# Attention and feed-forward kernel: third q, second x and third o put into the wait for the second chunk of w1, unread matmuls moved, work of batches 3 to 7 up to six slots sooner

## Chip, cores, metric

One core of one Trainium2 chip. The metric is the device time of one execution in microseconds (us); the median of several runs is quoted, with lowest and highest. The span of a profile is a little shorter than the time of the same run, so spans are compared with spans and times with times.

## The reference

```python
kv  = einsum('bhsd,bhse->bhde', k, v)              # 8 batches, 8 heads, 576 rows, d = 64
o   = einsum('bhsd,bhde->bhse', q, kv)
o   = o / sqrt(mean(o*o, -1) + 1e-6) * g_norm      # per head
x   = o.transpose(0, 2, 1, 3).reshape(8, 576, 512)
xn  = (x - mean(x)) / sqrt(var(x) + 1e-6) * g_ln
out = x + relu(xn @ w_ch1) @ w_ch2                 # w_ch1 512 x 2048, w_ch2 2048 x 512
```

## The kernel before

Almost all of the time is the two products with w_ch1 ("first product", line 401) and w_ch2 ("second product", line 417). Each main tile of 128 rows needs q turned (d on the partitions), o = q kv, square, sum, root, y, x, a centred and scaled x (xc), and xc turned, before the first product of its batch. All of that small work is hung on an agenda of slots: `tick()` is called at the start of each group of matmuls of the products, 16 slots for each product of a batch, and runs what is due. In the traces below the engines keep to the order in which the program emits their instructions, even where later work is ready (PE while it waits until 17.89 us, DVE with its evictions at 136.67 us in batch 4), so a slot decides what stands behind what. In the names used here y is o divided by its root, x is y times g_norm, and an eviction is DVE's step that reads a finished bank of the second product and writes the output tile (o_sb, line 422).

The opening of the span, with the unread matmuls (`fill`), put in so that PE has work where it would otherwise wait: In the first trace of before eight of the first 24 start about 427 ns apart and the others 216 ns apart; the record of a granted clock of 1.00 begins between the two, at 4.55 us.

```python
def turn_first(i, pool, tag):                 # q of tile i of batch 0 -> transposed
    tp = pool.tile([128, HP, 128], bf16, tag=tag, name="tp")
    n = turn_groups(tp, i, 0, H)
    nc.scalar.copy(qts[0][:, i, :, :n], tp[:, :, :n])

def fill(n):                                  # results are never read
    for _ in range(n):
        p1 = ps2.tile([128, 512], f32, tag="p2", name="p1")
        nc.tensor.matmul(p1, lhsT=fill_sb[:, :128], rhs=fill_sb, start=True, stop=True)
        del p1
# ... cut ...
fill(24)
kv_first()                                    # kv of batch 0, two halves of the heads
t = [main_tile(0, i) for i in range(4)]
# ... cut ...
half_turn(0); half_o(0, 0); half_turn(1); half_o(1, 0); half_o(0, 1)
# ... sums of squares, roots ...
t[0].o_g(ps1, "p1"); t[1].o_g(ps1, "p1")
fill(5)
t[0].x_g(); t[1].root()
# ... cut ...
halves_turn(0, halves_xc(0), ps_out, "ops")
t[1].x_g()
xc1 = list(halves_xc(1))
# ... cut ...
at(0, lambda: turn_first(2, ps_m, "misc"))              # third q
at(2, lambda: halves_turn(1, xc1, ps_out, "ops"))       # second x
at(2.1, o2); at(2.2, x2)                                # third tile
at(4, lambda: turn_first(3, ps_m, "misc"))
at(5, lambda: t[3].o()); at(5.5, x3)
at(6, lambda: t[2].turn(True))
# ... cut ...
at(11, lambda: t[3].turn(True))
```

The loads are issued in one queue in this order: v (two halves), q's lower half (two), first chunk of w1, q's upper half, then the second, third and fourth chunk of w1. The first chunk suffices for the group of 16 matmuls of slot 0; the group of slot 1 needs the second chunk, those of slots 2 and 3 the second x.

For the later batches (slots relative to s = 32 b, where the first product of batch b begins):

```python
for b in range(3, B):
    s = 32 * b                                # b = 3 has its own slots 47, 57, 57.5
    at(s - 60, lambda b=b: load_batch(b, qts[b - 1][...]))
    at(s - 39, lambda b=b: kv_of(b))
    at(s - 38, lambda b=b: turn_q_dma(b))     # pack q on DVE, transposing load
    for j in range(J):
        o = s - 28 + (0, 4, 9, 13)[j]
        plan_tile(o, lambda b=b, j=j: main_tile(b, j), o + 6, False)  # o; y, x, xc at o+2
    if b % 2:
        plan_tile(s - 8, lambda b=b: rem_tile(b), s - 2, False)
    at(s + 14, lambda b=b: rstd_of(b))
```

## Time and profile before

Time: 297.01 us median (296.92 to 297.04, 3 runs). The profiled run took 295.8 us.

| | before, first profile |
|---|---|
| span | 293.9 us |
| PE busy | 282.0 us, 96% |
| first product of batch 0 begins | 16.02 us |
| second product of batch 0 begins | 34.72 us |
| from there to the end | 259.17 us |

From the page of before (busy time with share and count by engine, then the granted clock in 40 slices of the span, 9 meaning 90% or more):

```profile
span 293.9 us, 5779 instructions
PE 282.0 (96%) x2296; PEld 159.7 (54%) x2321; DVE 149.9 (51%) x334; ACT 157.9 (54%) x342; POOL 40.8 (14%) x68
...
PEclk9999999999999999999999999999999999999999
```

PE is the limit, at full clock. Only its waits can be won. The timeline of PE in the opening (start us, duration us, engine, line, operation, output<-input, shapes, count, and in brackets the idle time ahead and what ended it):

```profile
14.96 0.68 PE L539 MATMUL tp<-identity,xc 128*128 128x128 bf16 x4 [1.49 <-DVE xc L530]
15.65 0.44 PE L183 MATMUL tp<-identity,q_in 64*64 64x64 bf16 x16
16.02 1.07 PE L401 MATMUL p<-xT_blk,w_sb 128*128 128x128 bf16 x16
17.89 1.07 PE L401 MATMUL p<-xT_blk,w_sb 128*128 128x128 bf16 x16 [0.80 <-DMA w_sb<-in_moe_w_ch_dram]
18.79 0.39 PE L539 MATMUL tp<-identity,xc 128*128 128x128 bf16 x4
19.90 0.38 PE L259 MATMUL o_ps<-kv_pack,qt 128*128 128x128 bf16 x4 [0.72 <-ACT xT_blk L540]
20.12 1.95 PE L401 MATMUL p<-xT_blk,w_sb 128*128 128x128 bf16 x32
...
34.72 4.48 PE L417 MATMUL p<-w_sb,m 128*128 128x512 bf16 x19
```

PE waits 0.80 us at 17.89 for the second chunk of w1, and right behind it does work that did not need that chunk: it turns the second x (18.79), waits 0.72 us for ACT, and makes the third o (19.90).

In the batches, DVE and PE around the second product of batch 4 show a wait that recurs in batches 3 to 7:

```profile
134.35 0.69 DVE L291 TENSOR_TENSOR y<-o_ps,inv 128x512 f32<-128x512 f32 x1
135.07 0.69 DVE L310 SCALAR_TENSOR_TENSOR x_blk<-y,g_norm_sb 128x512 f32<-128x512 f32 x1
...
136.00 0.75 DVE L320 SCALAR_TENSOR_TENSOR xc<-x_blk,st_blk,g_ln_sb 128x512 bf16<-128x512 f32 x1
136.67 1.40 DVE L422 SCALAR_TENSOR_TENSOR o_sb<-p,rstd,x_blk 128x512 f32<-128x512 f32 x2
```

```profile
137.47 1.02 PE L417 MATMUL p<-w_sb,m 128*128 128x512 bf16 x4 [0.46 <-DVE o_sb L422]
```

DVE works through y, x and xc of the next batch before it gets to two evictions (o_sb, line 422) in a row. The third tile of the second product needs the bank of the first one, so PE stands still for 0.46 us.

### The profile page before, as it was taken

How to read it: one execution, taken by the hardware profiler on the slowest of the kernel's cores; microseconds unless marked ns; L12 is line 12 of the kernel's file. 1: busy time of each engine (PE TensorE's matmuls, PEld its weight loads, DVE VectorE, ACT ScalarE, POOL GpSimd, SP SyncE). 2: the span in 40 equal slices, each digit the busy share in tenths (PEclk: the TensorE clock that was granted, in tenths of full speed). 3: DMA queues.
4: the chain of work that ended last, by engine and by line, in shares of the span. 5: the costliest groups of instructions: out<-in, count | busy, mean ns of one | idle time of the engine just before them, and what ended most of it. 6: DMA issues, size and time to landing. Idle time of an engine off the chain costs nothing.

```text
span 293.9 us, 5779 instructions
## 1 busy us (share of the span) xinstructions
PE 282.0 (96%) x2296; PEld 159.7 (54%) x2321; DVE 149.9 (51%) x334; ACT 157.9 (54%) x342; POOL 40.8 (14%) x68
## 2 busy tenths in 40 slices
PE   8779999999999999999999999999999999999995
PEld 3469855996569744444444444444444444444444
DVE  5747018936995766568246863692378600220022
ACT  3457755885569832782189327930694266017500
POOL 8523510022014000500050005000000000000000
PEclk9999999999999999999999999999999999999999
DMA  7999999459679935994899259987501520131033
GB/s 214 202 206 204 200 203 196 109 95 181 130 143 162 155 70 115 162 196 72 164 167 169 32 107 162 202 85 145 107 18 37 118 61 0 38 71 36 0 73 72
DMA packets 63290, 35.84 MB, mean 122 GB/s; under 512 B 30748, under 2 KB 58268, under 8 KB 63264
## 3 DMA queue, kind: packets, MB, share of 16 engines
q0 software_dynamic: 28016, 17.76, 43.0%
q1 hardware_dynamic: 34736, 16.99, 28.6%
q10 hardware_dynamic: 512, 0.72, 0.7%
q8 instruction: 18, 0.29, 0.4%
q14 instruction: 8, 0.07, 0.1%
HBM read 36.71 MB, written 9.44 MB: 157 GB/s over the span
## 4 chain that ended last, share of the span: by engine, by line
PE 70%; DVE 11%; ACT 6%; DMA 6%; issue 4%; POOL 1%; DVEq 0%; SPq 0%; POOLq 0%
PE p L401 37%; PE p L417 28%; DMA w_sb<-in_moe_w_ch_dram 4%; DVE x_blk L310 3%; DVE y L291 3%; PE kv_ps L234 2%; PE o_ps L259 2%; DMA qt<-q_p 2%; ACT m L404 2%; DVE o_sb L422 1%; DVE xc L320 1%; ACT sq L265 1%; ACT dev L328 1%; DVE ss L286 1%; ACT rms L296 1%
## 5 line engine op out<-in xcount | busy, mean ns | idle before, releaser
L401 PE MATMUL p<-xT_blk,w_sb 128*128 128x128 bf16 (+2 forms) x1015 | 131.2, 285 | 1.3 <-DMA w_sb<-in_moe_w_ch_dram 0.8
L417 PE MATMUL p<-w_sb,m 128*128 128x512 bf16 (+2 forms) x592 | 128.3, 367 | 2.6 <-DVE o_sb L422 0.9
L404 ACT ACTIVATE m<-p 128x512 bf16<-128x512 f32 x144 | 84.8, 596 | 59.1 <-PE p L401 57.7
L401 PEld LDWEIGHTS <-w_sb 128*128 128x128 bf16 x1024 | 78.6, 98 | 45.6 <-DMA w_sb<-in_moe_w_ch_dram 1.0
L417 PEld LDWEIGHTS <-m 128*128 128x128 bf16 x608 | 56.7, 98 | 61.4 <-issue 1.5
L422 DVE SCALAR_TENSOR_TENSOR o_sb<-p,rstd,x_blk 128x512 f32<-128x512 f32 (+2 forms) x38 | 26.9, 718 | 40.7 <-PE p L417 35.3
L328 ACT ACTIVATE dev<-x_blk,st_blk 128x512 f32<-128x512 f32 x36 | 25.8, 716 | 20.0 <-DVE st_blk L314 20.0
L286 DVE TENSOR_REDUCE ss<-sq 128x8 f32<-128x512 f32 x34 | 23.2, 682 | 25.8 <-ACT sq L265 25.7
L320 DVE SCALAR_TENSOR_TENSOR xc<-x_blk,st_blk,g_ln_sb 128x512 bf16<-128x512 f32 x34 | 25.6, 752 | 1.2
L291 DVE TENSOR_TENSOR y<-o_ps,inv 128x512 f32<-128x512 f32 x34 | 23.5, 692 | 3.4 <-DVE inv L303 0.5
L265 ACT ACTIVATE sq<-o_ps 128x512 f32<-128x512 f32 x34 | 20.2, 595 | 8.9 <-PE o_ps L259 8.9
L310 DVE SCALAR_TENSOR_TENSOR x_blk<-y,g_norm_sb 128x512 f32<-128x512 f32 x34 | 23.5, 692 | 1.2
L410 DVE RECIPROCAL rstd<-rstd 128x4 f32<-128x4 f32 x9 | 1.5, 172 | 39.7 <-ACT rstd L409 39.7
L303 DVE RECIPROCAL inv<-rms 128x8 f32<-128x8 f32 x36 | 7.2, 201 | 22.6 <-ACT rms L296 22.6
L98 POOL COPY gate<-qt 1x1 bf16<-1x1 bf16 x5 | 0.9, 178 | 122.2 <-DMA qt<-q_p 122.2
L296 ACT ACTIVATE rms<-ss,eps_sb 128x8 f32<-128x8 f32 x36 | 10.7, 297 | 9.3 <-DVE ss L286 8.6
L259 PEld LDWEIGHTS <-qt 128*128 128x128 bf16 (+1 forms) x152 | 9.9, 100 | 8.8 <-issue 2.5
L259 PE MATMUL o_ps<-kv_pack,qt 128*128 128x128 bf16 (+1 forms) x152 | 13.3, 220 | 0.8 <-ACT xT_blk L540 0.7
L196 PE MATMUL p<-fill_sb 128*128 128x512 bf16 x29 | 8.2, 445 | 1.2 <-DVE eps_sb L137 1.2
L237 ACT CAST kv_pack<-kv_ps 64x256 bf16<-64x256 f32 x7 | 2.6, 366 | 8.9 <-PE kv_ps L234 8.8
L328 ACT ACTIVATION_READ_ACCUMULATOR dev<-x_blk,st_blk 128x1 f32 x36 | 6.8, 189 | 0.0
L234 PEld LDWEIGHTS <-k_in 128*64 128x64 bf16 x280 | 5.4, 112 | 2.6 <-issue 2.5
(78 smaller groups left out, 119.8 us busy)
## 6 DMA issues: line engine op xcount, KB each, us to landing
out_dram<-o_sb SPq DMA_DIRECT2D x70, 128.0 KB, 2.4
w_sb<-in_moe_w_ch_dram POOLq DMA_DIRECT2D x8, 512.0 KB, 14.0
k_in<-in_k_dram POOLq DMA_DIRECT2D x7, 320.0 KB, 5.4
v_in<-in_v_dram POOLq DMA_DIRECT2D x7, 320.0 KB, 8.0
q_in<-in_q_dram POOLq DMA_DIRECT2D x7, 320.0 KB, 10.4
q_in<-in_q_dram POOLq DMA_DIRECT2D x8, 256.0 KB, 11.3
k_in<-in_k_dram POOLq DMA_DIRECT2D x7, 256.0 KB, 6.7
v_in<-in_v_dram POOLq DMA_DIRECT2D x7, 256.0 KB, 8.9
```

The source lines that it names most:

```text
L259: nc.tensor.matmul(flat[rows, hp * 128:(hp + 1) * 128], lhsT=lhsT_of(hp), rhs=kvp[:, hp, :], start=True, stop=True)
L265: nc.scalar.activation(self.sq_t, self.o_ps, func=AF.Square)
L286: nc.vector.tensor_reduce(self.ss, self.sq_t, axis=AX.X, op=ALU.add)
L291: nc.vector.tensor_mul(self.y_t, self.o_ps, self.inv().to_broadcast([128, H, D]))
L296: nc.scalar.activation(self.r, self.ss, func=AF.Sqrt, scale=1.0 / D, bias=eps_sb)
L310: nc.vector.scalar_tensor_tensor(x_blk[:, ts].rearrange("p (h d) -> p h d", h=H), in0=self.y_t, scalar=1.0, in1=g_norm_sb.to_broadcast([12 ...
L320: nc.vector.scalar_tensor_tensor(self.xc_t, in0=x_blk[:, self.ts], scalar=st[:, 1, self.ts:self.ts + 1], in1=g_ln_sb, op0=ALU.add, op1=ALU ...
L328: nc.scalar.activation(dev, x_blk[:, ts], func=AF.Square, bias=st[:, 1, ts:ts + 1], accum_out=st[:, 2, ts:ts + 1])
L401: nc.tensor.matmul(p1[:, i, :], lhsT=w1_sb[:, kk, de * 128:(de + 1) * 128], rhs=blk[2][:, kk, sl], start=(kk == 0), stop=(kk == nK - 1))
L404: nc.scalar.activation(m1[:, de0:de0 + per, sl], p1, func=AF.Relu)
L417: nc.tensor.matmul(p2[:, c0:c1], lhsT=m1s[b][:, de, ts * 128:(ts + 1) * 128], rhs=w2_sb[:, de, c0:c1], start=(de == 0), stop=(de == nDe - 1))
L422: nc.vector.scalar_tensor_tensor(o_sb[:, c0:c1], in0=p2[:, c0:c1], scalar=rstds[b][:, ts:ts + 1], in1=blks[b][0][:, ts, c0:c1], op0=ALU.mu ...
```

## The change

The intent: fill the wait for the second chunk of w1 with work that doesn't need it; take away the wait of o for ACT by giving the copies of q and x to different engines and o another pair of banks; move unread matmuls from the start to where PE waits; and let the small work of the next batch end before the evictions begin. The slots of batches 4 to 7 move by three to six, those of batch 3 by one to three (its remainder tile by six).

```diff
-    def turn_first(i, pool, tag):
+    def turn_first(i, pool, tag, copy=nc.scalar.copy):
...
-        nc.scalar.copy(qts[0][:, i, :, :n], tp[:, :, :n])
+        copy(qts[0][:, i, :, :n], tp[:, :, :n])
-    def fill(n):
+    def fill(n, pool=ps2, tag="p2"):
...
-    fill(24)
+    fill(18)
     kv_first()
-    t = [main_tile(0, i) for i in range(4)]
+    t = [main_tile(0, i, ps2, "p2") for i in range(4)]
...
     half_turn(0)
+    fill(2, ps_out, "ops")
     half_o(0, 0)
...
-    fill(5)
+    fill(8)
...
-    at(0, lambda: turn_first(2, ps_m, "misc"))
-    at(2, lambda: halves_turn(1, xc1, ps_out, "ops"))
-    at(2.1, o2)
-    at(2.2, x2)
+    at(1, lambda: turn_first(2, ps_m, "misc", nc.vector.tensor_copy))
+    at(1.1, lambda: halves_turn(1, xc1, ps_out, "ops"))
+    at(1.2, o2)
+    at(1.3, x2)
...
-    at(5.5, x3)
+    at(5.1, x3)
...
-    at(11, lambda: t[3].turn(True))
+    at(10, lambda: t[3].turn(True))
...                                            (batches 3 to 7)
-            at(s - 39, lambda b=b: kv_of(b))
-            at(s - 38, lambda b=b: turn_q_dma(b))
+        d = -41 if b == 3 else -45
+        at(s + d, lambda b=b: kv_of(b))
+        at(s + d + 1.7, lambda b=b: turn_q_dma(b))
-            o = s - 28 + (0, 4, 9, 13)[j]
+            o = s + d + (10 if b == 3 else 12) + 5 * j
-            plan_tile(s - 8, lambda b=b: rem_tile(b), s - 2, False)
+            plan_tile(s - 14, lambda b=b: rem_tile(b), s - 8, False)
```

More of the change, by code (lines that the diff above doesn't have):

```diff
@@ L186, in turn_groups @@
         return 64 * len(groups)
-    def turn_first(i, pool, tag):
+    def turn_first(i, pool, tag, copy=nc.scalar.copy):
         tp = pool.tile([128, HP, 128], bf16, tag=tag, name="tp")
         n = turn_groups(tp, i, 0, H)
-        nc.scalar.copy(qts[0][:, i, :, :n], tp[:, :, :n])
-    def fill(n):
+        copy(qts[0][:, i, :, :n], tp[:, :, :n])
+    def fill(n, pool=ps2, tag="p2"):
         for _ in range(n):
-            p1 = ps2.tile([128, 512], f32, tag="p2", name="p1")
+            p1 = pool.tile([128, 512], f32, tag=tag, name="p1")
             nc.tensor.matmul(p1, lhsT=fill_sb[:, :128], rhs=fill_sb, start=True, stop=True)
@@ L609 @@
     at(78, lambda: rstd_of(2))
-    at(47, lambda: load_batch(3, qts[2][:1, J, HP - 1, 127:]))
-    at(57, lambda: kv_of(3))
-    at(57.5, lambda: turn_q_dma(3))
     for b in range(3, B):
         s = 32 * b
-        if b > 3:
-            at(s - 60, lambda b=b: load_batch(b, qts[b - 1][:1, J, HP - 1, 127:]))
-            at(s - 39, lambda b=b: kv_of(b))
-            at(s - 38, lambda b=b: turn_q_dma(b))
+        at(47 if b == 3 else s - 60,
+           lambda b=b: load_batch(b, qts[b - 1][:1, J, HP - 1, 127:]))
+        d = -41 if b == 3 else -45
+        at(s + d, lambda b=b: kv_of(b))
+        at(s + d + 1.7, lambda b=b: turn_q_dma(b))
         for j in range(J):
-            o = s - 28 + (0, 4, 9, 13)[j]
+            o = s + d + (10 if b == 3 else 12) + 5 * j
             plan_tile(o, lambda b=b, j=j: main_tile(b, j), o + 6, False)
         if b % 2:
-            plan_tile(s - 8, lambda b=b: rem_tile(b), s - 2, False)
+            plan_tile(s - 14, lambda b=b: rem_tile(b), s - 8, False)
         at(s + 14, lambda b=b: rstd_of(b))
```

## The prediction

> **What bounds the kernel now.** The page shows PE busy 282.0 of 293.9 us, DVE and ACT near half; the chain of waits is 70% PE. In the timeline sixteen 512-column matmuls take 3.45 us, 215.7 ns each[...]. The granted clock is 1.00 in every window. So only places where PE waits can be won. From the timeline and PE's waits:
> - 17.89 us: the second chunk of w1 lands at 17.84; 0.80 us idle.
> - 19.90: o of the third tile waits 0.72 us for the ACT copy of x.
> - 23.5, 24.8, 31.1: 0.1 to 0.2 us each.
> - batches 3 to 7: a matmul of the second product waits for the eviction (line 422, DVE) at 107.3, 137.5, 167.5, 197.8, 227.9: about 0.2, 0.4, 0.2, 0.4, 0.2 us. DVE runs y, x, xc of the next batch ahead of that eviction. Two waits for transposed q, 0.1 and 0.2 us (118.7, 179.0).
>
> **What the change does.**
> 1. Third q (0.37 us), second x (0.25) and o (0.22) move into the wait for the second chunk of w1. The copies are split: q on DVE (about 0.5 us, from 0.49 for two halves, behind xc, which ends at 17.32), x on ACT. I expect o at about 17.9 and the second chunk at 17.9 to 18.2; it cannot start before 17.84. The next chunk starts at about 19.0 instead of 20.12: **1.1 us**, plus **0.4** of the small waits at 23.5, 24.8 and 31.1 (x of tile 3 turned one slot sooner). Later chunks of w1 landed at 20.39 and 23.02; they will be needed at about 21.2 and 23.6, the last of w2 (landed 42.67) at 43.3. Close, but enough.
> 2. Six fewer unread matmuls: 6 x 0.216 = 1.3 us of PE, worth **0**. The second half of kv starts at 8.97 because v lands at 8.93; the q turns at 9.74 and 10.75 follow landings at 9.70 and 10.62. The 2 + 3 added lie in waits of 0.35 and 1.49 us.
> 3. Batches 3 to 7 sooner: the next batch's last y, x, xc end before the first eviction, so the waits of line 422 go, about **1.3 us**, and the q waits, **0.2**. k and v still land well before kv in batches 4 to 7; for batch 3 the margin is about 1 us. ACT gets more inside the first product, and around 88 to 92 us its roots wait for a full DVE: minus **0.3** for new PE waits.
>
> Sum: 1.1 + 0.4 + 1.3 + 0.2 - 0.3 = 2.7 us, perhaps 3, of 297.0: about 1%. Predicted **294.1 us**, range **293.0 to 295.4** (8 in 10). Faster by over 2%: 0.03; within 2%: 0.96; slower by over 2%: 0.01.
>
> **What would show each step.** Timeline: second chunk of w1 at 17.9 to 18.2, the next straight behind it; second product at about 33.2 instead of 34.72; kv's second half still at about 8.97. Waits: no line 417 on line 422 after 100 us; 29.9 to 30.0 us per batch instead of 30.2.
>
> **What would make it wrong.** DVE's copy of q comes late and o blocks PE beyond 18.2; later chunks of w1 or w2 become the wait; kv of batch 3 waits for v; ACT, in order, holds up the relus until PE runs out of banks[...].

## The result

| | before | after |
|---|---|---|
| time, median | 296.97 us (295.85 to 297.04, 4 runs) | 293.45 us (292.89 to 294.47, 4 runs) |
| ratio | 1 | 0.9894 (95% interval 0.9857 to 0.9931) |
| span of the profile | 293.9 us | 292.7 us |
| second half of v landed | 8.93 us | 10.41 us |
| second product of batch 0 begins | 34.72 us | 34.75 us |
| from there to the end | 259.17 us | 257.94 us |

The kernel is 1.1% faster, inside the predicted range, and by the 2% criterion the same.

The page of after:

```profile
span 292.7 us, 5775 instructions
PE 281.8 (96%) x2294; PEld 159.4 (54%) x2320; DVE 150.8 (52%) x335; ACT 154.7 (53%) x341; POOL 40.7 (14%) x68
...
PEclk9999999999999999999999999999999999999999
```

The opening of after, PE timeline, the lines that answer to those of before:

```profile
16.41 0.68 PE L540 MATMUL tp<-identity,xc 128*128 128x128 bf16 x4 [0.84 <-DVE xc L531]
17.16 1.34 PE L401 MATMUL p<-xT_blk,w_sb 128*128 128x128 bf16 x16
18.43 0.44 PE L183 MATMUL tp<-identity,q_in 64*64 64x64 bf16 x16
18.80 0.40 PE L540 MATMUL tp<-identity,xc 128*128 128x128 bf16 x4
19.40 0.40 PE L259 MATMUL o_ps<-kv_pack,qt 128*128 128x128 bf16 x4 [0.20 <-DVE qt L191]
19.63 2.84 PE L401 MATMUL p<-xT_blk,w_sb 128*128 128x128 bf16 x48
...
34.75 4.48 PE L417 MATMUL p<-w_sb,m 128*128 128x512 bf16 x19
```

The new order is as meant: no wait for w1 is left, q, x and o go ahead of its second chunk, and the next two groups follow without a gap (48 matmuls in a row). Yet the second product begins no sooner than before. Everything is late by about 1.4 us from the start, and in this run v landed at 8.39 and 10.41 us instead of 7.48 and 8.93 (landings of the loads in the trace); that the one causes the other is shown further down, by after_again and after_vlate.

In the batches, DVE and PE at the same place of batch 4:

```profile
133.67 0.75 DVE L320 SCALAR_TENSOR_TENSOR xc<-x_blk,st_blk,g_ln_sb 128x512 bf16<-128x512 f32 x1
134.87 0.75 DVE L422 SCALAR_TENSOR_TENSOR o_sb<-p,rstd,x_blk 128x512 f32<-128x512 f32 x1 [0.45 <-PE p L417]
```

```profile
130.30 2.75 PE L417 MATMUL p<-w_sb,m 128*128 128x512 bf16 x12
132.98 0.88 PE L234 MATMUL kv_ps<-v_in,k_in 128*64 128x64 bf16 x40
134.02 6.21 PE L417 MATMUL p<-w_sb,m 128*128 128x512 bf16 x28 [0.16 <-issue]
```

Now DVE waits for PE at the eviction and not the other way round. No matmul waits on line 422 any more.

So the two profiles differ by 1.2 us, all of it in the batches, while the medians differ by 3.5 us. Two profiles out of eight runs did not tell where the rest was. I had three explanations: the parts simply add and the opening's gain is hidden by a late v in this profile (A); the unread matmuls matter after all (B); or the opening gained nothing (C).

### The profile page after: what moved, and what is told of

Its sections match the earlier page's. It is cut to its first block, busy times and chain, and to the rows that moved or that the text cites. A ratio compares the mean times of both kernels' runs of the same rounds, so it can differ in the third digit from the quotient of the medians.

```text
span 292.7 us, 5775 instructions
## 1 busy us (share of the span) xinstructions
PE 281.8 (96%) x2294; PEld 159.4 (54%) x2320; DVE 150.8 (52%) x335; ACT 154.7 (53%) x341; POOL 40.7 (14%) x68
## 4 chain that ended last, share of the span: by engine, by line
PE 81%; DMA 7%; DVE 5%; ACT 2%; issue 2%; SPq 1%; POOL 0%; POOLq 0%
PE p L401 40%; PE p L417 34%; DMA qt<-q_p 4%; DMA v_in<-in_v_dram 3%; PE o_ps L259 2%; PE kv_ps L234 2%; DVE o_sb L422 1%; DVE ss L286 1%; DMA out_dram<-o_sb 1%; DVE x_blk L310 1%; DVE y L291 1%; ACT m L404 1%; PE tp L183 1%; ACT xT_blk L338 1%; PE p L196 1%
## 5 line engine op out<-in xcount | busy, mean ns | idle before, releaser
L417 PE MATMUL p<-w_sb,m 128*128 128x512 bf16 (+2 forms) x589 | 126.9, 368 | 1.6 <-issue 0.8
L338 ACT COPY xT_blk<-tp 128x512 bf16<-128x512 bf16 x10 | 5.8, 579 | 2.3 <-PE tp L336 2.3
## 6 DMA issues: line engine op xcount, KB each, us to landing
v_in<-in_v_dram POOLq DMA_DIRECT2D x7, 256.0 KB, 10.4
```

Of the source, the lines that this page charges most:

```text
L417: nc.tensor.matmul(p2[:, c0:c1], lhsT=m1s[b][:, de, ts * 128:(ts + 1) * 128], rhs=w2_sb[:, de, c0:c1], start=(de == 0), stop=(de == nDe - 1))
```

## The experiments

In each job the kernel before ran in the same rounds on the same chip (11 runs in each of three jobs; medians 297.10, 296.82 and 296.77 us). "Full clock" below means a mean granted clock of 0.997 or more in that run.

### batches_only and opening_only: the change in two parts

batches_only is before with only the new slots of batches 3 to 7; opening_only is after with the old slots:

```diff
 # batches_only = before, and
-        at(s - 39, kv_of) ... o = s - 28 + (0, 4, 9, 13)[j] ... rem_tile at s - 8
+        at(s + d, kv_of)  ... o = s + d + 12 + 5 * j        ... rem_tile at s - 14
 # opening_only = after, and the same lines the other way round
```

> The opening of before with the earlier slots for batches 3 to 7. Theory A (the two parts add; the opening's gain is hidden in the after profile only because v landed late there): 1.0 to 1.5 us faster than before, 295.6 to 296.0 in the state where before takes 297.0; the matmul waits on line 422 after 100 us are gone. Rival C (the opening gains nothing; the batches made all of it): 2.5 to 3.5 us faster, 293.5 to 294.5.

Measured: correct, 295.16 us median (294.28 to 296.85, 6 runs), ratio 0.9938 (0.9900 to 0.9975). In its trace the part from the second product on takes 257.79 us, against 259.17 before, and the waits on line 422 are gone. The runs fall into groups that go with the clock: 294.28 and 294.34 at full clock, 295.98 at 0.993, 296.83 and 296.85 at 0.987 (the profiled one took 294.30 at 0.992: its half-clock stretch, 11.49 to 14.91 us, lay ahead of the wait for w1, and its second product began at 34.73 us as in the first profile of before).

> The new opening (order and fills) with the old slots for batches 3 to 7. Theory A: 1.3 to 1.9 us faster than before, 295.1 to 295.7; in its profile the start of the second product minus the landing of v's second half is 24.3 to 24.5 us as in after (34.75 - 10.41), not 25.8 as in before (34.72 - 8.93). Rival C: within 0.4 us of before.

Measured: correct, 294.61 us median (294.54 to 295.40, 6 runs), ratio 0.9916 (0.9891 to 0.9941), full clock in all 6. Second product at 33.32 us, v's second half at 8.97, so 24.35 us after it, as theory A asked; 259.13 us from there on. C falls: the opening gains 1.4 us in the trace. But 2.5 us at the median is more than A allowed, and again a clock is involved.

### fills_only and after_oldfills: the unread matmuls alone

```diff
 # fills_only = before, and
-    fill(24)
+    fill(18)
+    fill(2, ps_out, "ops")      # behind half_turn(0)
-    fill(5)
+    fill(8)
 # after_oldfills = after with 24, 0 and 5
```

> Before with 18, 2 and 8 unread matmuls in place of 24, 0 and 5, nothing else. Theory A: within 0.3 us of before, since v and q set the starts behind the fills. Rival B (24 fills reach past the landing of v when the PE clock rises late, as in the after profile with 11 slow matmuls instead of 8): 0.4 us or more faster.

Measured: correct, 295.78 us median, and all 6 runs within 295.74 to 295.88; before in the same rounds 297.10 (295.79 to 298.29); ratio 0.9950 (0.9926 to 0.9974). The lowest run of before, at full clock, took 295.79. So the unread matmuls do not make the best run faster; they take away the slow ones. Full clock in all 6 runs, in before in one of 11.

> After with the old 24, 0 and 5 unread matmuls. Theory A: within 0.3 us of after, 293.2 to 293.8, 3 us or so faster than before. Rival B: 0.4 us or more slower than after.

Measured: correct, 294.02 us median (292.89 to 296.19, 6 runs), ratio 0.9906. Three runs at full clock, 292.89 to 293.61; three at 0.994 or less, 294.42 to 296.19. The size is that of rival B, but its reason, that 24 reach past the landing of v, was not tested by this yet.

### fills_first, fills_later, fills_eight: which of them

```diff
 # fills_first = before with 18, 0, 5;  fills_later = before with 24, 2, 8
 # fills_eight = before with 24, 0, 8
```

> Before with 18 unread matmuls first in place of 24, the rest as before. Theory D (the gain of fills_only is a PE clock that no longer drops, and the 2 and 8 later matmuls hold it): like before, 296.7 to 298.3 in most runs with a mean clock of 0.986 to 0.994. Rival E (24 were too many at the start, they delayed kv): 295.7 to 295.9 in all runs, clock 0.998 or more.

Measured: correct, 297.45 us median (295.99 to 298.17, 6 runs), ratio 1.0009 (0.9970 to 1.0048), no run at full clock (0.988 to 0.994). Fewer at the start alone is worth nothing. Rival E falls.

> Before with 24, 2 and 8 unread matmuls in place of 24, 0 and 5. Theory D: 295.7 to 296.0 in nearly all runs with a clock of 0.998 or more, as fills_only. Rival E: like before, 296.7 to 298.3.

Measured: correct, 295.89 us median (295.70 to 296.85, 6 runs), ratio 0.9967 (0.9930 to 1.0004), five of six at full clock. That is five of six against three of 11 for before in the same rounds, and none of six for fills_first: the later ones do it. The interval of the time itself still reaches 1.

> Before with 24, 0 and 8 unread matmuls in place of 24, 0 and 5. Theory D1 (the stretch before xc, busy 0.53 in the second trace of before, is what lowers the clock, so the 8 alone hold it): 295.7 to 296.0 with clock 0.998 or more in nearly all runs. Theory D2 (the 2 are needed as well): several runs at 296.7 or more with clock 0.994 or less.

Measured: correct, 295.83 us median (295.80 to 296.81, 6 runs), ratio 0.9979 (0.9952 to 1.0006), four of six at full clock, against four of 11 for before in the same rounds. With six runs four of six can be told neither from four of 11 nor from five of six, so whether the eight do it alone, do part of it, or need the two stays open.

### before_again: a second trace of before

> Before, unchanged, for a second trace of it. Theory D: if its time is 296.7 or more, the trace shows one or two stretches of 3.4 us at half clock between 8 and 19 us, and the second product starts 1 to 2.5 us later than 34.72; the rest of the span is 259.1 to 259.2 us as in the first trace. If it takes 295.8 the clock is full throughout and nothing is learned.

Measured: correct, 297.03 us, mean clock 0.992. Its windows (stretch and length in us, PE busy and count, granted clock, DMA share, GB/s):

```profile
10.27:13.68 3.41, 2.82 (x71) 1.00 1.31 202
13.68:17.09 3.41, 1.81 (x28) 1.00 1.26 207
17.09:20.51 3.42, 3.42 (x34) 0.50 1.24 206
20.51:23.92 3.41, 2.89 (x59) 1.00 1.24 207
```

and four lines of its PE timeline, the first of them the last seven of the 24 unread matmuls:

```profile
7.66 1.67 PE L196 MATMUL p<-fill_sb 128*128 128x512 bf16 x7
...
15.80 0.68 PE L539 MATMUL tp<-identity,xc 128*128 128x128 bf16 x4 [1.49 <-DVE xc L530]
...
16.79 3.40 PE L401 MATMUL p<-xT_blk,w_sb 128*128 128x128 bf16 x32
...
21.36 1.95 PE L401 MATMUL p<-xT_blk,w_sb 128*128 128x128 bf16 x32
```

This is the typical run of before. From 17.09 us the clock is halved for 3.4 us; the first two groups of the first product, 32 matmuls, take 3.40 us where the next 32 take 1.95 at full clock. The stretch ahead of it had PE busy for 1.81 of 3.41 us: in it lies the wait of 1.49 us for xc behind the five unread matmuls. The second product begins at 35.95 instead of 34.72 us, and the rest of the span is 259.18 us, unchanged. The trace of fills_first shows two such stretches, 6.83 us from 17.07 on, and its second product begins at 36.95.

Two things happen in before_again, and only one of them costs. The clock first rose at 6.86 us instead of 4.55, so the 24 unread matmuls ran to 9.33 us although v's second half had landed at 8.79, and xc came 0.84 us later than in the first trace: that is what rival B had foreseen. But in the old order the wait for w1 takes such a delay up. In batches_only, which has the same opening, v landed 0.81 us late and the first product began at 16.98 us, still later than the 16.79 here, and its second product came at 34.73. So the 1.2 us between 34.73 and 35.95 belong to the slow stretch inside the first product.

With eight unread matmuls there, after (trace of after_again, below) has no busy share that low, and no halved clock:

```profile
8.05:11.46 3.41, 2.69 (x89) 1.00 1.30 202
11.46:14.88 3.42, 2.66 (x20) 1.00 1.33 202
14.88:18.29 3.41, 2.81 (x46) 1.00 1.24 207
```

The 33 runs of before in the three jobs sort by clock: eight at full clock take 295.71 to 295.96 us, 18 at 0.992 to 0.994 take 296.70 to 297.55, and seven at 0.988 take 298.18 to 298.78. One stretch of 3.41 us at half clock lowers a mean over 295 us by 0.5 x 3.41 / 295 = 0.006, two by 0.012, which fits the two lower groups. With 18, 2 and 8 unread matmuls and v loaded as in after, all 33 runs (after, after_again, after_actcopy, after_qsooner, opening_only, fills_only) were at full clock.

### after_again and after_vlate: the late v

```diff
 # after_vlate = after, and
-    nc.gpsimd.dma_start(v_p[:, HP // 2:], pairs(v, HP // 2, HP))     # ahead of q
+    nc.gpsimd.dma_start(v_p[:, HP // 2:], pairs(v, HP // 2, HP))     # behind q's lower half
```

> After, unchanged, as the yardstick of this chip and a second trace. Full clock (0.997 or more) in every run. If v's second half lands at about 8.9 us: 292.9 to 293.1 us and the second product at 33.3 to 33.4; if it lands later, later by nearly the same.

Measured: correct, 293.23 us median (293.00 to 293.85, 6 runs), ratio 0.9884 (0.9856 to 0.9912), full clock in all six. In its trace (run of 293.00 us) v's second half lands at 8.89 us. PE in the opening:

```profile
14.98 0.68 PE L540 MATMUL tp<-identity,xc 128*128 128x128 bf16 x4 [0.83 <-DVE xc L531]
15.73 1.34 PE L401 MATMUL p<-xT_blk,w_sb 128*128 128x128 bf16 x16
17.00 0.44 PE L183 MATMUL tp<-identity,q_in 64*64 64x64 bf16 x16
17.37 0.40 PE L540 MATMUL tp<-identity,xc 128*128 128x128 bf16 x4
17.97 0.40 PE L259 MATMUL o_ps<-kv_pack,qt 128*128 128x128 bf16 x4 [0.20 <-DVE qt L191]
18.20 2.84 PE L401 MATMUL p<-xT_blk,w_sb 128*128 128x128 bf16 x48
...
33.32 2.97 PE L417 MATMUL p<-w_sb,m 128*128 128x512 bf16 x13
```

This is the profile to hold against the first one of before: both at full clock, both with v at 8.9 us. o is at 17.97 us (19.90 before), the second chunk of w1 is used from 18.20, and the next two groups follow at once. The second product begins at 33.32 us, 1.40 us sooner, and 257.90 us follow instead of 259.17, 1.27 less.

> After with the load of v's second half issued behind the two loads of q's lower half instead of ahead of them, so that it lands last of the three, at about 10.5 us; the first chunks of w1 land as before. Theory F (what separates the runs of after from each other is when v lands): 1.0 to 1.6 us slower than after_again where that one's v lands at 8.9, second product at 34.4 to 34.9 as in the first trace of after, the rest of the span unchanged at 257.8 to 257.9. Rival: the opening has slack for v, under 0.4 us slower.

Measured: correct, 295.19 us median (294.45 to 295.90, 6 runs), ratio to before 0.9945 (0.9918 to 0.9972). In its trace v's second half lands at 10.51 us, w1's second chunk at 17.75 (17.74 in after_again), the second product begins at 34.85, and 258.02 us follow. At full clock (two runs, 294.45 and 294.64) it is 1.3 us slower than after_again. So the opening of after has no slack for v: 1.6 us later at v is 1.5 us later at the second product, as between the two traces of after (1.5 and 1.4). Not foreseen: in the other four runs the mean clock was 0.992 to 0.994, although the unread matmuls were the new ones. With v loaded later the drop came back; where it fell is not known, since the trace kept is of a run without it.

### after_actcopy: the engine of the copy of q

```diff
-    at(1, lambda: turn_first(2, ps_m, "misc", nc.vector.tensor_copy))
+    at(1, lambda: turn_first(2, ps_m, "misc"))                        # ACT
```

> After with the copy of the third q on ACT again, in its new place. On ACT it stands behind the relu of the first chunk and ahead of the copies of the second x: I expect o ready at about the same time but x later by 0.5 us, so the chunk behind w1's second one waits: 0.2 to 0.5 us slower than after (293.1 to 294.0 at full clock). If the engine of that copy makes no difference: 292.9 to 293.5.

Measured: correct, 293.37 us median (293.22 to 293.75, 6 runs), full clock in all, on another chip than after_again (293.23). In the trace o waits 0.5 us for ACT's copy of q where it waits 0.20 for DVE's, and the second product begins at 33.59 instead of 33.32 us. So the copy on DVE is worth about 0.3 us in the trace, within what I expected; my detail was wrong: o was held up, not x. The times alone would not resolve it. The other pair of banks for o was never run without the new order, so what it adds is not shown.

### after_qsooner: a further step

After, q of the later batches still arrives late at times. Packing it right behind kv, ahead of the remainder tile on DVE:

```diff
-        at(s + d + 1.7, lambda b=b: turn_q_dma(b))
+        at(s + d + 0.9, lambda b=b: turn_q_dma(b))
```

> After with the packing and transposing load of q of batches 3 to 7 right behind kv, ahead of y, x, xc of the remainder tile. Should remove the two waits of o for q (0.2 us each at 114.7 and 203.8): rest of the span 257.4 to 257.6 instead of 257.8 to 257.9, time 0.2 to 0.4 us below after_again. If the packing delays the evictions, waits on line 422 return and it is slower.

Measured: correct, 292.61 us median (292.57 to 293.20, 5 runs), ratio to before 0.9864 (0.9836 to 0.9891). From the second product on 257.41 us, as expected, against 257.79 to 258.02 in the six other traces with the new slots, and line 422 holds up no matmul of the second product. On the same chip the median is 0.6 us below after_again. That is 0.2%, the ranges overlap by one run, and the trace is the better evidence. It is the fastest version.

## Why the prediction was right, and where it was wrong

The time was right: 294.1 us forecast, 293.45 measured, range 293.0 to 295.4. It was right partly by luck, because one term was wrong and the base to which I applied the sum was another state than the one the sum was read from. Both made the forecast too high; a late v in at least one of the four runs of after (294.47 us) made the measured time higher too.

1. **Order of the opening: right.** I forecast 1.1 + 0.4 us, o at about 17.9, the second chunk at 17.9 to 18.2, the second product at about 33.2 us. The trace of after_again has 17.97, 18.20 and 33.32, a gain of 1.40 us; opening_only has the same 33.32. w1's later chunks and w2 did not become waits. "DVE's copy of q comes late" was real but small: 0.20 us.

2. **Unread matmuls: wrong.** The step that failed is "Six fewer unread matmuls: 6 x 0.216 = 1.3 us of PE, worth **0**", with its last sentence "The 2 + 3 added lie in waits of 0.35 and 1.49 us". The landings I cited set those starts in the first trace, not in before_again, where the 24 ran past v's landing; still, fewer at the start alone are worth nothing (fills_first). But I took the filled waits to cost and give nothing. Most runs of before have the mean clock of one or two stretches of 3.41 us at half clock, and the traces that caught them (before_again, fills_first, batches_only) have them in the opening; in the rounds of fills_only none of its 6 runs has such a mean, and 10 of 11 of before have. fills_only is 1.3 us faster at the median, with the same best run (295.74 and 295.79 us). I never took a falling clock for something that before suffered from.

3. **The base: wrong.** "The granted clock is 1.00 in every window" was true of the profile and not of the kernel. The profiled run took 295.8 us and the timed ones 296.92 to 297.04. That difference was on the page in front of me. I subtracted 2.7 us, "perhaps 3", read from a run at full clock, from 297.0. From 295.8 the 2.7 give 293.1 us, and after at full clock with v on time takes 293.0, the lower edge of my range. This and point 2 are one omission seen from two sides: a base of 297.0 needs a gain from the unread matmuls, a base of 295.8 needs none.

4. **Batches 3 to 7: right in sum.** I forecast 1.3 + 0.2 - 0.3 = 1.2 us; the traces give 1.27 (257.90 against 259.17), and batches_only alone gives the same. The waits on line 422 went. The new wait that I feared at 88 to 92 us is there: 0.21 us at 91.83, behind a root that ACT could not begin before 89.33. "and the q waits, **0.2**" was wrong: o still waits 0.1 to 0.2 us for q at 114.7 and 203.8 us in the first trace of after; only after_qsooner removed them.

5. **What I did not foresee: v.** The opening of after shifts with v's landing nearly one to one, and v landed at 10.4 us in the first profile of after. Why it lands late in some runs stays open; the core's DMA moved 209 GB/s over the first 10.5 us in both first traces.

What stays open besides: the condition under which the clock drops. Busy share alone does not decide it. The stretch before the drop had PE busy for 53% in before_again and fills_first and 60% in batches_only; the trace of after_vlate has a stretch of 51% (1.76 of 3.42 us) without a drop. Two leads lie in the traces, and no run was made to test either. The drops begin a whole number of 3.41 us after the clock's first rise (17.09 - 6.86 is three of them, 11.49 - 4.67 two), and that rise lies anywhere from 4.29 to 7.08 us in the 14 traces. Counted in stretches of 3.41 us from the rise, the same wait of 1.49 us is cut differently from run to run: in the first trace of before it fell into the stretch from 11.38 to 14.79 us, which had 2.03 us busy, and no drop came. And what PE does may count, not only whether it is busy: without the turns (products with the identity) it was busy for 0.94 us ahead of the drop in before_again and fills_first, the least of the first eight stretches of any trace; the next are 1.21 us, without a drop. The stretch ahead of the drop in batches_only has 1.79 us, but 1.51 of them in 64x64 matmuls. What is shown is the frequency: 13 of 46 runs at full clock with 24, 0 and 5 unread matmuls (before in the three jobs, before_again, batches_only, after_oldfills), 33 of 33 with 18, 2 and 8 while v is loaded first.

## What to carry to other kernels

Compare the time of the profiled run with the timed runs before reading the profile as the kernel's: a gap of 1 us here meant another clock state (0.992 to 0.994 against 0.997 or more in the runs of before), and no line of that profile could show it. Work that nobody reads was worth more than a microsecond here when part of it lay in waits (1.3 us at the median, fills_only), and nothing was lost or won by fewer of it at the start alone (ratio 1.0009, fills_first); look at the mean clock of every run, not at one trace, to see it. And when two parts of a change are judged, compare traces with the same state of the inputs (here v landed, clock full): then the parts added to within 0.2 us (1.5 us of span for opening_only and 1.4 for batches_only, whose half-clock stretch cost nothing, against 2.7 for after_again).
